# Retention, MoE and SOLU on one core: integer addition and subtractions of the weight conversion on VectorE, the activation as a maximum taken from PSUM

## The chip, the cores and the metric

One core of one Trainium2 chip runs the whole program. TensorE (PE in the profile) multiplies matrices into PSUM; VectorE (DVE), ScalarE (ACT) and GpSimd (POOL) do the elementwise work, and SyncE (SP) issues the transfers. The metric is the device time of one execution in microseconds. A time is a median of several runs.

## The reference, cut to what matters

Three layers follow each other on 3072 tokens of width 512:

```
# retention, 8 heads of 64: a decaying state per head, token by token
state = gamma * state + k_t v_t^T ;  y_t = scale * q_t state
# first feed-forward layer, d_ff 2048
h = x @ w_in
g = where(h >= 1, h, where(h <= -1, 0, (h + 1)**2 / 4))
x = g @ w_out
# second feed-forward layer, d_ff 1024
h = x @ w_in ;  u = h * softmax(h)
out = (layernorm(u) * g_ln) @ w_out
```

The weights come as float64. The kernel turns each weight tile into two float32r parts whose sum is the value, and each product of a weight and an activation is made of three matmuls (high by high, low by high, high by low).

## The kernel before, in words

The program has two phases. Phase A computes retention and the first feed-forward layer together: the 3072 tokens make 8 blocks of 384, and d_ff makes 16 parts of 128, so there are 128 slots (block, part). A slot is `moe_h` (12 matmuls of 384 columns into a PSUM tile `hp`, L325), the activation, and two slots later `moe_out` (12 matmuls into `acc`, L360). Retention (`attention`) goes in between, in steps that a table assigns to slots. Phase B is the second feed-forward layer, 24 tiles of 128 tokens (`h2p`, `tp`, `op`).

Weights are converted in phase A. A weight tile arrives as 128 partitions by 512 float64 (`w_raw`), and `conv_w` makes `m` (tile `wm`) and `p` (tile `wp`) of its two words. ACT takes the high word (L139), DVE clips it (L140), shifts it (L143) and puts the sign in (L144, from `w_raw` and `wm`); ACT makes `p` from the low word (L142); then `m` and `p` are added as 32-bit integers (L145), ACT rounds the sum to the high part (L149), and the low part is the difference (L150). Eight of the last 16 tiles are scaled on the way (L147). There are 48 tiles: 32 for the first layer, taken up over slots 0 to 26 or so, and 16 for the second layer, during the last block of phase A. The choice of engine for L150 is `lo_eng`: of the 48 differences, 14 are on DVE (`LO_I`, `LO_O`) and 34 on POOL; all 48 integer additions are on POOL.

The activation of a slot works on 128x384 values: DVE clips `hp` to -1..1 (L337), ACT makes `rr`, the part of `hp` above 1 (L338), ACT squares the clipped value (L339, half plus half of it), DVE adds the two (L340, `cs` and `rr`, both in SBUF), and `split` rounds the sum on ACT (L121, `gh`) and takes the rest on DVE (L122, `gl`). `hp` is read by L337 and L338; there are two such PSUM tiles, so a slot's `hp` has to be free again when the second slot after it begins.

Order: the program is written in slots, and a list scheduler (a timeline simulation at build time) settles each engine's order from it by priority and readiness. Each engine then runs its own queue in that order and waits on semaphores. So a change of one instruction can move many others.

Of the kernel before, what the change touches and what calls it, by code (L numbers as in the profile page):

```python
# [9 lines left out]
F32 = mybir.dt.float32  # L10
F32R = mybir.dt.float32r
U32 = mybir.dt.uint32
I32 = mybir.dt.int32
AF = mybir.ActivationFunctionType
ALU = mybir.AluOpType
AX = mybir.AxisListType

B, H, S, D = 4, 8, 768, 64
# [8 lines left out]
BLK = 384  # L27
# [3 lines left out]
NF = FF // 128  # L31
NF2 = FF2 // 128
NTILE = NT // 128
# words of the high half of a float64, read as float32: 2^-127 and the largest float32r
LO_I = (0,1)
LO_O = range(4,16)
LO_2 = 0
# [25 lines left out]
C_ACT = 0  # L63
# [10 lines left out]
def kernel(  # L74
# [16 lines left out]
    order = ExitStack()  # L91
    if DMA_ORDER > -99:
        order.enter_context(tc.manual_schedule(engines={mybir.EngineType.SP}))
    ve, sc, gp, pe = nc.vector, nc.scalar, nc.gpsimd, nc.tensor
# [12 lines left out]
    neg1 = const.tile([128, 1], F32, tag="neg1", name="neg1")  # L107
    mask = const.tile([128, 1, C], F32, tag="mask", name="mask")
    half = const.tile([128, 1], F32, tag="half", name="half")
# [4 lines left out]
    def fl(t):  # L114
        return t.bitcast(F32)
# [5 lines left out]
            sc.activation(hi, src, AF.Copy)  # L121
        (lo_eng or ve).tensor_tensor(out=lo, in0=src, in1=fl(hi), op=ALU.subtract)  # L122

# [1 line left out]
    wi, wo = {}, {}  # L125
    state = {}

# [5 lines left out]
    def conv_w(raw, scale=None, lo_eng=None):  # L133
        lw, hw = raw[:, :, 0], raw[:, :, 1]
        m = cv.tile([128, 512], F32, tag="wm", name="wm", bufs=WM_BUFS)
        p = cv.tile([128, 512], F32, tag="wp", name="wp", bufs=WP_BUFS)
        mu, mi = m.bitcast(U32), m.bitcast(I32)
        # the high word, cut to the range of float32, gives sign, exponent and 20 bits
        sc.activation(m, hw.bitcast(F32), AF.Abs)  # L139
        ve.tensor_scalar(m, m, W_MIN, W_MAX, op0=ALU.max, op1=ALU.min)  # L140
        # the low word, rounded to the last 3 bits, lies in the bits of a float32 of 2 upwards
        sc.activation(p, lw, AF.Copy, bias=2.0, scale=2.0 ** -51)  # L142
        ve.tensor_scalar(mu, mu, 3, None, op0=ALU.logical_shift_left)  # L143
        ve.scalar_tensor_tensor(mu, hw, 0x80000000, mu, op0=ALU.bitwise_and, op1=ALU.bitwise_xor)  # L144
        gp.tensor_tensor(out=mi, in0=mi, in1=p.bitcast(I32), op=ALU.add)  # L145
        if scale is not None:
            ve.tensor_scalar(m, m, scale, None, op0=ALU.mult)  # L147
        w = wp.tile([128, 2, 512], F32R, tag="w", name="w")
        sc.activation(w[:, 0, :], m, AF.Copy)  # L149
        (lo_eng or gp).tensor_tensor(out=w[:, 1, :], in0=m, in1=fl(w[:, 0, :]), op=ALU.subtract)  # L150
        return w[:, 0, :], w[:, 1, :]

# [1 line left out]
    # Heads go in pairs (even, odd); the even one takes partitions 0-63 of queries, keys and  # L154
    # state, the odd one 64-127, and TensorE works on both halves of its array at a time.
    # In x the halves of pairs 2 and 3 are swapped, and so are the rows of w_in.
    def attention(u, env):
        b, c = divmod(u, NCH)
        first, last = c == 0, c == NCH - 1
# [94 lines left out]
                gp.tensor_tensor(out=d, in0=d, in1=g, op=ALU.mult)  # L254

    w2i, w2o = {}, {}
# [1 line left out]
    ve.memset(neg1, -1.0)  # L258
    ve.memset(half, 0.5)
    ve.memset(mask, 1.0)  # L260
# [2 lines left out]
    moe = ctx.enter_context(tc.tile_pool(name="moe", bufs=2))  # L263
# [6 lines left out]
    env = {"attp": attp, "xp": xp, "x": {}}  # L270
    GB = 3

    # Phase A goes over (block, part of d_ff) in an order that takes up new weights at half the
    # rate at first, while they are converted; a block's sum may be put aside in DRAM between.
    segs = [(0, 0, SA), (1, 0, SB), (0, SA, NF), (1, SB, NF)] + [(b, 0, NF) for b in range(2, NBLK)]
    slots = [(b, f, f == f0, f == f1 - 1, f0 == 0, f1 == NF)
             for (b, f0, f1) in segs for f in range(f0, f1)]
# [2 lines left out]
        base.setdefault(b, n)  # L280
        first_use.setdefault(f, n)

    # slot -> units of attention that take a step in it
    sched = {}
    for u in range(NU):
        blk, k = divmod(u, CPB)
        x = (k - 3, SA - 3 + k, X2 + 3 * k)[blk] if blk < 3 else base[blk] - NF + PER * k + SHIFT
        at = (x - STEP0, x - 2, x - 1, x) if u < NF32 else (x - 5, x - 3, x - 2, x - 2, x - 1, x)
# [29 lines left out]
    def moe_h(blk, f):  # L318
        xh, xl = env["x"][blk]
        hp = ps_h.tile([128, 512], F32, tag="h", name="hp")[:, :BLK]  # L320
        wh, wl = wi[f]
        n = 0
        for (l, r) in ((wh, xh), (wl, xh), (wh, xl)):
            for k in range(KD):
                pe.matmul(hp, l[:, k * 128:(k + 1) * 128], r[:, k, :], start=(n == 0), stop=(n == 3 * KD - 1))  # L325
                n += 1
        cs = moe.tile([128, BLK], F32, tag="cs", name="cs")
        rr = moe.tile([128, BLK], F32, tag="rr", name="rr", bufs=1)
        gh = moe.tile([128, BLK], F32R, tag="gh", name="gh", bufs=GB)
        gl = moe.tile([128, BLK], F32R, tag="gl", name="gl", bufs=GB)  # L330
        if blk < C_ACT:
            sc.activation(cs, hp, AF.Relu, bias=half, scale=0.5)
            sc.activation(rr, hp, AF.Relu, bias=neg1)
            ve.tensor_scalar(cs, cs, 1.0, None, op0=ALU.min)
            sc.activation(cs, cs, AF.Square)
        else:
            ve.tensor_scalar(cs, hp, -1.0, 1.0, op0=ALU.max, op1=ALU.min)  # L337
            sc.activation(rr, hp, AF.Relu, bias=neg1)  # L338
            sc.activation(cs, cs, AF.Square, bias=half, scale=0.5)  # L339
        ve.tensor_tensor(out=cs, in0=cs, in1=rr, op=ALU.add)  # L340
        split(cs, gh, gl)
        return gh, gl

# [61 lines left out]
    for s, slot in enumerate(slots):  # L405
        blk, f = slot[:2]
# [22 lines left out]
    while pend:  # L429
        moe_out(*pend.pop(0))  # L430

# [1 line left out]
    if True:  # L433
        ident = bp.tile([128, 128], F32, tag="ident", name="ident", bufs=1)
        nc.sync.dma_start(ident, ident_d)
# [20 lines left out]
        def h2(t):  # L456
            hi, lo = x2s.pop(t)
            pool, tag = ((ps_a, "pa"), (ps_acc, "acc"))[1 if PSV else t % 2]
            hps = [pool.tile([128, 512], F32, tag=tag, name="h2p") for _ in range(2)]
            for n in range(2):  # L460
                m = 0
                for (l, part) in ((hi, 0), (hi, 1), (lo, 0)):
                    for k in range(KD):
                        pe.matmul(hps[n], l[:, k, :], w2i[k, n][part], start=(m == 0), stop=(m == 3 * KD - 1))  # L464
                        m += 1
            st = bp.tile([128, 16], F32, tag="st", name="st", bufs=4)
            e = wp.tile([128, 2, 512], F32, tag="w", name="e")
            u = wp.tile([128, 2, 512], F32, tag="w", name="u")
            bn = bp.tile([128, 2, 6], F32, tag="bn", name="bn")
            for n in range(2):  # L470
                ve.tensor_reduce(st[:, n:n + 1], hps[n], axis=AX.X, op=ALU.max)
            ve.tensor_scalar(st[:, 2:3], st[:, 0:1], st[:, 1:2], -1.0, op0=ALU.max, op1=ALU.mult)
            for n in range(2):
                sc.activation(e[:, n, :], hps[n], AF.Exp, bias=st[:, 2:3], accum_out=st[:, 3 + n:4 + n])
            for n in range(2):
                ve.tensor_tensor(out=u[:, n, :], in0=hps[n], in1=e[:, n, :], op=ALU.mult)
                ve.bn_stats(bn[:, n, :], u[:, n, :])
            ve.bn_aggr(st[:, 6:8], bn)
            ve.tensor_scalar(u, u, st[:, 6:7], None, op0=ALU.subtract)
            # f = r / sqrt(r^2 var + eps), r = 1 / (sum + 1e-9)  # L480
            ve.tensor_scalar(st[:, 8:9], st[:, 3:4], st[:, 4:5], 1e-9, op0=ALU.add, op1=ALU.add)
            ve.reciprocal(st[:, 9:10], st[:, 8:9])
            ve.tensor_scalar(st[:, 10:11], st[:, 7:8], st[:, 9:10], st[:, 9:10], op0=ALU.mult, op1=ALU.mult)
            ve.tensor_scalar(st[:, 10:11], st[:, 10:11], 1e-6, None, op0=ALU.add)
            # 1 / sqrt by Newton's steps from a first guess off the exponent
            si = st.bitcast(I32)
            ve.tensor_scalar(si[:, 11:12], si[:, 10:11], 1, None, op0=ALU.arith_shift_right)
            ve.tensor_scalar(si[:, 11:12], si[:, 11:12], -1.0, float(0x5F3759DF), op0=ALU.mult, op1=ALU.add)
            for _ in range(4):
                ve.tensor_scalar(st[:, 13:14], st[:, 10:11], st[:, 11:12], st[:, 11:12], op0=ALU.mult, op1=ALU.mult)  # L490
                ve.tensor_scalar(st[:, 13:14], st[:, 13:14], -0.5, 1.5, op0=ALU.mult, op1=ALU.add)
                ve.tensor_scalar(st[:, 11:12], st[:, 11:12], st[:, 13:14], None, op0=ALU.mult)
            ve.tensor_scalar(st[:, 12:13], st[:, 11:12], st[:, 9:10], None, op0=ALU.mult)
            ust[t] = (u, st)
# [103 lines left out]
```

## Time and profile before

| what | value |
|---|---|
| median of 3 runs | 972.96 us (972.27 to 973.82) |
| span of the profiled execution | 969.7 us |
| PE busy | 936.3 us, 97% |
| DVE busy | 741.9 us, 77% |
| ACT busy | 455.6 us, 47% |
| POOL busy | 201.0 us, 21% |

The profile holds one execution. Its span runs from its first to its last instruction; its own time outside the profiler was not recorded, and the median of the runs is 3.3 us above the span (start and end of the program), so times below are the span plus 3.3 us. Busy time is an average over stages with different limits, which is why the rows below are taken by stage.

### The profile page before, as it was taken

The numbers are of one execution on the slowest core, as the hardware profiler recorded it, in microseconds if no ns is written. First come the engines' busy times: TensorE is split into PE (matmuls) and PEld (weight loads), VectorE is DVE, ScalarE is ACT, GpSimd is POOL, SyncE is SP. The second block draws the span as 40 slices with busy tenths as digits, with TensorE's granted clock in tenths as the row PEclk, the third lists the DMA queues.
The fourth block names the chain that finished last, engine by engine and source line by source line (L and its number), as shares of the span: only waits on it lengthen the run. The fifth ranks groups of instructions, "written<-read, shape, count | busy, mean of one in ns | idle before, by whom it ended". The sixth has DMA issues, their size and how long they took to land.

```text
span 969.7 us, 14961 instructions
## 1 busy us (share of the span) xinstructions
PE 936.3 (97%) x5560; PEld 856.5 (88%) x5560; DVE 741.9 (77%) x1593; ACT 455.6 (47%) x905; POOL 201.0 (21%) x177
## 2 busy tenths in 40 slices
PE   8798898999999999999999999989999999999998
PEld 7588888999999999999999999969888888888886
DVE  6999999877666666655664574997788888888885
ACT  3557676545545545544553464664433333333322
POOL 2754544212211221111220120662000000000000
PEclk9899999999999999999999999999999999999999
DMA  9902823154233232420320230311111011010000
GB/s 366 360 1 82 250 82 114 48 169 126 79 98 116 92 97 80 128 77 22 114 72 12 107 143 1 122 64 69 66 55 42 35 55 54 23 61 28 22 23 33
DMA packets 31465, 87.03 MB, mean 90 GB/s; under 512 B 4384, under 2 KB 10656, under 8 KB 31392
## 3 DMA queue, kind: packets, MB, share of 16 engines
q1 hardware_dynamic: 31392, 86.08, 26.9%
q8 instruction: 44, 0.72, 0.3%
q14 instruction: 29, 0.24, 0.1%
HBM read 71.90 MB, written 14.16 MB: 89 GB/s over the span
## 4 chain that ended last, share of the span: by engine, by line
PE 74%; DVE 18%; issue 3%; ACT 2%; DMA 2%; SPq 0%; POOL 0%; ACTq 0%; DVEq 0%; POOLq 0%
PE acc L360 19%; PE hp L325 19%; PE h2p L464 14%; PE op L516 14%; DVE wm L144 3%; DVE cs L340 3%; DVE wm L140 2%; PE pv L233 2%; PE tp L505 2%; DVE gl L122 2%; PE qp L206 2%; DVE wm L143 2%; DVE cs L337 2%; PE pv L229 2%; DVE w L150 1%
## 5 line engine op out<-in xcount | busy, mean ns | idle before, releaser
L360 PE MATMUL acc<-gh,w 128*128 128x384 f32 x1024 | 214.3, 339 | 9.6 <-ACT gh L121 7.6
L325 PE MATMUL hp<-xh,w 128*128 128x384 f32 x1024 | 209.6, 340 | 5.6 <-ACT rr L338 3.9
L360 PEld LDWEIGHTS acc<-gh,w 128*128 128x128 f32 x1024 | 180.1, 189 | 15.4 <-ACT gh L121 10.4
L325 PEld LDWEIGHTS hp<-xh,w 128*128 128x128 f32 x1024 | 179.0, 189 | 12.2 <-ACT rr L338 6.2
L338 ACT ACTIVATE rr<-hp,neg 128x384 f32<-128x384 f32 x128 | 74.1, 579 | 161.4 <-DVE cs L337 161.2
L340 DVE TENSOR_TENSOR cs<-cs,rr 128x384 f32<-128x384 f32 x128 | 86.0, 672 | 77.7 <-ACT cs L339 76.8
L360 PE MATMUL acc<-gl,w 128*128 128x384 f32 x512 | 121.7, 338 | 4.8 <-DVE gl L122 4.8
L325 PE MATMUL hp<-xl,w 128*128 128x384 f32 x512 | 111.8, 338 | 0.0
L122 DVE TENSOR_TENSOR gl<-cs,gh 128x384 fp32r<-128x384 f32 x128 | 85.5, 668 | 26.7 <-ACT gh L121 24.5
L121 ACT ACTIVATE gh<-cs 128x384 fp32r<-128x384 f32 x128 | 66.8, 522 | 65.7 <-DVE cs L340 65.5
L464 PE MATMUL h2p<-w,x2h 128*128 128x512 f32 x384 | 97.4, 395 | 0.0
L360 PEld LDWEIGHTS acc<-gl,w 128*128 128x128 f32 x512 | 90.3, 188 | 8.1 <-DVE gl L122 7.5
L337 DVE TENSOR_SCALAR cs<-hp 128x384 f32<-128x384 f32 x128 | 70.5, 551 | 32.3 <-PE hp L325 31.8
L325 PEld LDWEIGHTS hp<-xl,w 128*128 128x128 f32 x512 | 91.7, 190 | 0.5 <-DVE xl L122 0.3
L516 PE MATMUL op<-w,lh 128*128 128x512 f32 x384 | 91.4, 390 | 0.2 <-ACT lh L121 0.2
L145 POOL TENSOR_TENSOR wm<-wm,wp 128x512 int32<-128x512 int32 x48 | 69.1, 1440 | 88.0 <-DVE wm L144 70.6
L516 PEld LDWEIGHTS op<-w,lh 128*128 128x128 f32 x384 | 71.9, 188 | 15.4 <-ACT lh L121 0.5
L464 PEld LDWEIGHTS h2p<-w,x2h 128*128 128x128 f32 x384 | 70.5, 188 | 13.5
L339 ACT ACTIVATE cs<-cs,half 128x384 f32<-128x384 f32 x128 | 77.6, 606 | 2.5 <-DVE cs L337 2.5
L150 POOL TENSOR_TENSOR w<-wm,w 128x512 fp32r<-128x512 f32 x34 | 49.6, 1461 | 52.2 <-ACT w L149 51.9
L211 POOL TENSOR_SCALAR_AFFINE_SELECT sm<-sm 128x512 f32<-128x512 f32 x36 | 36.3, 1010 | 99.6 <-DVE sm L210 99.6
L254 POOL TENSOR_TENSOR state<-state,gdec 64x256 f32<-64x256 f32 x32 | 22.0, 688 | 165.1 <-DVE state L253 163.9
(79 smaller groups left out, 1299.7 us busy)
## 6 DMA issues: line engine op xcount, KB each, us to landing
qk<-in_qk_t_dram SPq DMA_DIRECT2D x72, 256.0 KB, 3.8
kv<-in_kv_t_dram SPq DMA_DIRECT2D x24, 512.0 KB, 3.8
w_raw<-in_w_in_dram SPq DMA_DIRECT2D x24, 512.0 KB, 7.3
w_raw<-in_w_out_dram SPq DMA_DIRECT2D x24, 512.0 KB, 6.7
x2d<-xs SPq DMA_DIRECT2D x32, 192.0 KB, 2.0
x2r<-x2d SPq DMA_DIRECT2D x8, 768.0 KB, 4.3
out_dram<-o SPq DMA_DIRECT2D x24, 256.0 KB, 2.0
qn<-in_qk_t_dram SPq DMA_DIRECT2D x15, 256.0 KB, 3.1
```

Source lines behind the costliest of these rows:

```text
L121: sc.activation(hi, src, AF.Copy)
L122: (lo_eng or ve).tensor_tensor(out=lo, in0=src, in1=fl(hi), op=ALU.subtract)
L145: gp.tensor_tensor(out=mi, in0=mi, in1=p.bitcast(I32), op=ALU.add)
L150: (lo_eng or gp).tensor_tensor(out=w[:, 1, :], in0=m, in1=fl(w[:, 0, :]), op=ALU.subtract)
L325: pe.matmul(hp, l[:, k * 128:(k + 1) * 128], r[:, k, :], start=(n == 0), stop=(n == 3 * KD - 1))
L337: ve.tensor_scalar(cs, hp, -1.0, 1.0, op0=ALU.max, op1=ALU.min)
L338: sc.activation(rr, hp, AF.Relu, bias=neg1)
L339: sc.activation(cs, cs, AF.Square, bias=half, scale=0.5)
L340: ve.tensor_tensor(out=cs, in0=cs, in1=rr, op=ALU.add)
L360: pe.matmul(acc[d][:, :BLK], l[:, d * 128:(d + 1) * 128], r, start=(first and m == 1), stop=(last and m == 3))
L464: pe.matmul(hps[n], l[:, k, :], w2i[k, n][part], start=(m == 0), stop=(m == 3 * KD - 1))
L516: pe.matmul(op, l[:, f, :], w2o[f][part], start=(n == 0), stop=(n == 3 * NF2 - 1))
```

## The change

The integer addition L145 and the remaining subtractions L150 are issued on DVE in place of POOL. In the activation, `rr` goes away with its ACT instruction, and the last step becomes a maximum of `hp`, read from PSUM, and the squared value. (For h above 1 the squared value is 1 and the maximum is h; below -1 it is 0; in between the square is never below h.) The branch on `C_ACT`, which is 0, was never taken before and is gone. All else in the diff is comments.

```
-        gp.tensor_tensor(out=mi, in0=mi, in1=p.bitcast(I32), op=ALU.add)
+        ve.tensor_tensor(out=mi, in0=mi, in1=p.bitcast(I32), op=ALU.add)
         if scale is not None:
             ve.tensor_scalar(m, m, scale, None, op0=ALU.mult)
         w = wp.tile([128, 2, 512], F32R, tag="w", name="w")
         sc.activation(w[:, 0, :], m, AF.Copy)
-        (lo_eng or gp).tensor_tensor(out=w[:, 1, :], in0=m, in1=fl(w[:, 0, :]), op=ALU.subtract)
+        ve.tensor_tensor(out=w[:, 1, :], in0=m, in1=fl(w[:, 0, :]), op=ALU.subtract)
...
         cs = moe.tile([128, BLK], F32, tag="cs", name="cs")
-        rr = moe.tile([128, BLK], F32, tag="rr", name="rr", bufs=1)
...
-            ve.tensor_scalar(cs, hp, -1.0, 1.0, op0=ALU.max, op1=ALU.min)
-            sc.activation(rr, hp, AF.Relu, bias=neg1)
-            sc.activation(cs, cs, AF.Square, bias=half, scale=0.5)
-        ve.tensor_tensor(out=cs, in0=cs, in1=rr, op=ALU.add)
+        ve.tensor_scalar(cs, hp, -1.0, 1.0, op0=ALU.max, op1=ALU.min)
+        sc.activation(cs, cs, AF.Square, bias=half, scale=0.5)
+        ve.tensor_tensor(out=cs, in0=hp, in1=cs, op=ALU.max)
         split(cs, gh, gl)
```

Eight lines less stand above, so in the changed program L337, L339 and L340 are L331, L332 and L333, and what stood at L360 is at L353.

In DVE's queue, around the fifth to seventh slot of phase A (before: the conversion of `wm_925` and `wm_975`, with slot work between), the rows read:

```order
L140 TENSOR_SCALAR wm_925<-wm_925 128x512
L337 TENSOR_SCALAR cs_809<-hp_796 128x384
L143 TENSOR_SCALAR wm_925<-wm_925 128x512
L122 TENSOR_TENSOR gl_754<-cs_751,gh_753 128x384
L144 SCALAR_TENSOR_TENSOR wm_925<-w_raw_736,wm_925 128x512
L140 TENSOR_SCALAR wm_975<-wm_975 128x512
L143 TENSOR_SCALAR wm_975<-wm_975 128x512
L340 TENSOR_TENSOR cs_809<-cs_809,rr_810 128x384
L144 SCALAR_TENSOR_TENSOR wm_975<-w_raw_792,wm_975 128x512
```

and in the changed program at about the same place (`wm_543` and `wm_636` are two tiles in conversion; `wp` is their other word):

```order
L143 TENSOR_SCALAR wm_636<-wm_636 128x512
L144 SCALAR_TENSOR_TENSOR wm_543<-w_raw_389,wm_543 128x512
L150 TENSOR_TENSOR w_488<-wm_480,w_488 128x512
L144 SCALAR_TENSOR_TENSOR wm_636<-w_raw_413,wm_636 128x512
L333 TENSOR_TENSOR cs_660<-hp_647,cs_660 128x384
L145 ISA wm_543<-wm_543,wp_544 128x1024
L145 ISA wm_636<-wm_636,wp_637 128x1024
L122 TENSOR_TENSOR gl_662<-cs_660,gh_661 128x384
L150 TENSOR_TENSOR w_551<-wm_543,w_551 128x512
L150 TENSOR_TENSOR w_644<-wm_636,w_644 128x512
```

Additions and differences now stand in DVE's queue between the other steps, a few places behind the step that feeds them. The addition is built as another instruction than before: it goes over 1024 elements of two bytes in place of 512 of four. The last step of the activation reads `hp`.

In POOL's queue the same stretch of the program reads, before:

```order
L145 TENSOR_TENSOR wm_925<-wm_925,wp_926 128x512
L145 TENSOR_TENSOR wm_975<-wm_975,wp_976 128x512
L150 TENSOR_TENSOR w_933<-wm_925,w_933 128x512
L145 TENSOR_TENSOR wm_986<-wm_986,wp_987 128x512
L150 TENSOR_TENSOR w_994<-wm_986,w_994 128x512
L145 TENSOR_TENSOR wm_1034<-wm_1034,wp_1035 128x512
```

and in the changed program POOL holds only retention's own steps there:

```order
L183 TENSOR_TENSOR kv_307<-kv_307,vdec_88 128x512
L254 TENSOR_TENSOR state_105<-state_105,gdec_89 64x4x64 x2
L183 TENSOR_TENSOR kv_1336<-kv_1336,vdec_88 128x512
L211 AFFINE_SELECT sm_1474<-sm_1474 128x512
L211 AFFINE_SELECT sm_1552<-sm_1552 128x512
L183 TENSOR_TENSOR kv_1492<-kv_1492,vdec_88 128x512
```

The 82 instructions of the conversion have left this queue, and 82 have come into DVE's.

## Rows read from the trace of the kernel before

**Rows 1.** Busy us (and instructions) of each engine by stage of the span.
```profile
core 0: us, PE busy (x) PEld busy (x) DVE busy (x) ACT busy (x) POOL busy (x), PEclk, DMA share, GB/s
...
25.00:185.00 160.00, 142.37 (x837) 128.98 (x838) 153.30 (x228) 102.34 (x193) 81.70 (x61) 0.96 0.41 138
...
200.00:590.00 390.00, 389.50 (x2593) 378.12 (x2592) 250.20 (x458) 193.67 (x394) 70.99 (x74) 1.00 0.31 94
...
616.00:668.00 52.00, 45.36 (x239) 40.59 (x238) 50.18 (x69) 32.46 (x59) 32.25 (x22) 1.00 0.27 99
...
700.00:970.00 270.00, 265.97 (x1264) 221.75 (x1264) 222.69 (x715) 83.16 (x178) 0.00 (x0) 1.00 0.11 39
```

**Rows 2.** Groups on DVE from 25 to 185 us: count, busy us, mean ns.
```profile
L144 DVE SCALAR_TENSOR_TENSOR wm<-w_raw,wm 128x512 uint32<-128x512 uint32 x30 | 25.6, 854 | 0.2
L122 DVE TENSOR_TENSOR gl<-cs,gh 128x384 fp32r<-128x384 f32 x26 | 22.1, 851 | 2.4 <-ACT gh L121 2.3
L340 DVE TENSOR_TENSOR cs<-cs,rr 128x384 f32<-128x384 f32 x26 | 20.8, 801 | 2.8 <-ACT cs L339 2.7
L143 DVE TENSOR_SCALAR wm<-wm 128x512 uint32<-128x512 uint32 x29 | 20.6, 713 | 0.2
L140 DVE TENSOR_SCALAR wm<-wm 128x512 f32<-128x512 f32 x29 | 19.1, 663 | 0.1
L150 DVE TENSOR_TENSOR w<-wm,w 128x512 fp32r<-128x512 f32 x14 | 15.8, 1129 | 0.0
...
L199 DVE TENSOR_TENSOR kh<-qk,kh 64x512 fp32r<-64x512 f32 x7 | 5.8, 843 | 0.2
L122 DVE TENSOR_TENSOR xl<-xt,xh 128x512 fp32r<-128x512 f32 x4 | 5.0, 1252 | 0.0
L200 DVE TENSOR_TENSOR qs<-qk,qs 128x512 fp32r<-128x512 f32 x5 | 4.6, 923 | 0.1
```

**Rows 3.** Timeline of DVE from 106 us: start us, duration us.
```profile
106.06 0.68 DVE L144 SCALAR_TENSOR_TENSOR wm<-w_raw,wm 128x512 uint32<-128x512 uint32 x1
106.66 0.41 DVE L140 TENSOR_SCALAR wm<-wm 128x512 f32<-128x512 f32 x1
107.11 1.38 DVE L143 TENSOR_SCALAR wm<-wm 128x512 uint32<-128x512 uint32 x1
108.53 1.67 DVE L144 SCALAR_TENSOR_TENSOR wm<-w_raw,wm 128x512 uint32<-128x512 uint32 x1
...
111.88 0.68 DVE L150 TENSOR_TENSOR w<-wm,w 128x512 fp32r<-128x512 f32 x1
112.61 0.56 DVE L122 TENSOR_TENSOR gl<-cs,gh 128x384 fp32r<-128x384 f32 x1
...
114.11 0.43 DVE L143 TENSOR_SCALAR wm<-wm 128x512 uint32<-128x512 uint32 x1
```

**Rows 4.** Timeline of POOL in the same stretch.
```profile
106.91 1.30 POOL L145 TENSOR_TENSOR wm<-wm,wp 128x512 int32<-128x512 int32 x1 [1.78 <-ACT w L149]
108.17 1.48 POOL L150 TENSOR_TENSOR w<-wm,w 128x512 fp32r<-128x512 f32 x1
```

**Rows 5.** Groups over the whole span: DVE steps that read PSUM, and ACT's `rr`.
```profile
L337 DVE TENSOR_SCALAR cs<-hp 128x384 f32<-128x384 f32 x128 | 70.5, 551 | 32.3 <-PE hp L325 31.8
...
L338 ACT ACTIVATE rr<-hp,neg 128x384 f32<-128x384 f32 x128 | 74.1, 579 | 161.4 <-DVE cs L337 161.2
...
L373 DVE TENSOR_TENSOR xs<-acc,xs 128x384 f32<-128x384 f32 x8 | 4.3, 552 | 3.4 <-DMA xs<-x2p 2.5 <-PE qp L206 1.0
```

**Rows 6.** Groups on POOL from 25 to 185 us.
```profile
L145 POOL TENSOR_TENSOR wm<-wm,wp 128x512 int32<-128x512 int32 x30 | 43.1, 1439 | 55.1 <-DVE wm L144 42.9 <-ACT cs L339 8.3 <-ACT w L149 1.8
L150 POOL TENSOR_TENSOR w<-wm,w 128x512 fp32r<-128x512 f32 x18 | 26.4, 1465 | 9.7 <-ACT w L149 9.5
```

**Rows 7.** Groups on POOL from 616 to 668 us.
```profile
L150 POOL TENSOR_TENSOR w<-wm,w 128x512 fp32r<-128x512 f32 x12 | 17.7, 1474 | 6.0 <-ACT w L149 5.9
L145 POOL TENSOR_TENSOR wm<-wm,wp 128x512 int32<-128x512 int32 x10 | 14.8, 1481 | 12.0 <-DVE wm L144 12.0
```

More of the change, by code (lines that the diff above doesn't have):

```diff
@@ L327, in moe_h @@
         cs = moe.tile([128, BLK], F32, tag="cs", name="cs")
-        rr = moe.tile([128, BLK], F32, tag="rr", name="rr", bufs=1)
         gh = moe.tile([128, BLK], F32R, tag="gh", name="gh", bufs=GB)
         gl = moe.tile([128, BLK], F32R, tag="gl", name="gl", bufs=GB)
-        if blk < C_ACT:
-            sc.activation(cs, hp, AF.Relu, bias=half, scale=0.5)
-            sc.activation(rr, hp, AF.Relu, bias=neg1)
-            ve.tensor_scalar(cs, cs, 1.0, None, op0=ALU.min)
-            sc.activation(cs, cs, AF.Square)
-        else:
-            ve.tensor_scalar(cs, hp, -1.0, 1.0, op0=ALU.max, op1=ALU.min)
-            sc.activation(rr, hp, AF.Relu, bias=neg1)
-            sc.activation(cs, cs, AF.Square, bias=half, scale=0.5)
-        ve.tensor_tensor(out=cs, in0=cs, in1=rr, op=ALU.add)
+        ve.tensor_scalar(cs, hp, -1.0, 1.0, op0=ALU.max, op1=ALU.min)
+        sc.activation(cs, cs, AF.Square, bias=half, scale=0.5)
+        ve.tensor_tensor(out=cs, in0=hp, in1=cs, op=ALU.max)
         split(cs, gh, gl)
```

## The prediction

> **What bounds the kernel now.** I read the windows by stage first, because the page's averages (PE 97%, DVE 77%) hide that the bound changes along the span. From 200 to 590 us PE is busy 389.5 of 390 us and DVE 250 [rows 1]: there PE's matmuls set the time and nothing that this change does to DVE, ACT or POOL can show. From 700 us on POOL does nothing, DVE is busy 222.7 and PE 266.0 of 270 us [rows 1]; the change touches no instruction there. Two stages are different. From 25 to 185 us, while the first layer's weights are converted, DVE is busy 153.3 of 160 us and PE only 142.4; from 616 to 668 us, while the second layer's are, DVE is busy 50.2 of 52 us and PE 45.4 [rows 1]. In both DVE sets the pace, so the question is whether DVE gets more or less to do in these 212 us.
>
> At first sight more: 82 instructions come to the engine that is full. But the groups on DVE show that it is full of something else. One conversion step, L143, takes 713 ns in the mean between 25 and 185 us, L150 takes 1129 [rows 2]; the timeline shows the same forms at 0.43 and 0.68 us where they run free [rows 3]. The long ones can be matched: L143 begins at 107.11 and takes 1.38 us, while POOL's L145 runs from 106.91 to 108.21; L144 begins at 108.53 and takes 1.67 us, while POOL's L150 runs from 108.17 to 109.65 [rows 3, 4]. So they end about 0.3 to 0.55 us after POOL's end, as if most of their work began only then. The DVE forms that read PSUM keep their price with POOL busy or not: L337 551 ns, L373 552 [rows 5]. A POOL instruction of 1.44 us [rows 6] thus costs DVE time too.
>
> **The change, part by part.**
>
> Stretch before, 25 to 185 us: count by (mean less free duration), from [rows 2] and [rows 3], with 0.68 us for all two-source forms of 512, 0.56 for those of 384, 0.43 for L143, 0.41 for L140. L144 30 x 0.174 = 5.2; L122 `gl` 26 x 0.291 = 7.6; L340 26 x 0.241 = 6.3; L143 29 x 0.283 = 8.2; L140 29 x 0.253 = 7.3; L150 14 x 0.449 = 6.3; L199, `xl` and L200 together 7 x 0.163 + 4 x 0.572 + 5 x 0.243 = 4.6. Sum 45.5 us, in a stage of 160.
>
> What goes: POOL is busy 81.7 us there [rows 1], of which the additions and differences are 43.1 + 26.4 = 69.5 [rows 6]. The rest, 12.2 us or 15%, is retention's and stays. If the stretch follows POOL's time, 6.8 us stay and 38.7 go.
>
> What comes: 30 additions and 18 differences [rows 6]. A difference is known: 0.68 us [rows 3]. In the queue a step of this size puts the next one off by 0.60 us where that one does not depend on it (106.06 to 106.66), and by 0.73 us at worst (111.88 to 112.61) [rows 3]; I take 0.60, since the changed queue alternates between tiles. The addition has no row: it is built as another instruction, over 1024 elements of two bytes. Lower bound: it moves the same bytes as a two-source form of 512 words, 0.68 us. Upper bound: it goes at the pace of single elements; from 384 to 512 elements a two-source form grows from 0.56 to 0.68 us [rows 3], so 0.94 ns each, and 1024 take 0.68 + 0.48 = 1.16 us; POOL's own 1.44 us [rows 6] is further off. I take 0.68, since the fast forms (L140: 512 words in 0.41) show that DVE need not spend a step per element, and it is the row of the same bytes. 48 x 0.60 = 28.8 us.
>
> The Trainium skill, VectorE: DVE Perf Modes, section "Mode 2×_1P", says that two-source forms of 16-bit elements go two per cycle; with the 151 cycles at 0.96 GHz that the page puts on top of a two-source addition, an estimate for 1024 is 0.69 us, and the sum would stay as it is. No row of this trace has a two-byte form of that kind.
>
> Net in this stage: DVE's demand falls by 38.7 - 28.8 = 9.9 us. Not all of it comes back as time: DVE's 153.3 then stands at 143, beside PE's 142.4, and two engines so close wait for each other in turn. I take seven tenths, 7 us. If each step costs 0.73 instead, 38.7 - 35.0 = 3.7 us are left.
>
> From 616 to 668 us: POOL is busy 32.25 us, all conversion [rows 1, 7]. At the first stage's ratio (45.5 / 81.7 = 0.56) that is 18 us of stretch, and all of it goes. 10 additions and 12 differences come [rows 7]: 22 x 0.60 = 13.2 us. Net 4.8 us less; PE's idle 52 - 45.4 = 6.6 us is the ceiling. I take 4.
>
> The activation: ACT loses 128 `rr` of 579 ns, 74 us [rows 5]. ACT is busy 102 of 160 and 32 of 52 us [rows 1], so that is no time by itself; in the two stages it shortens the way from `hp` to `gh` by one instruction, which DVE's in-order queue mostly covers with conversion work. From 200 to 590 us PE's 389.5 of 390 us cover it wholly. The new last step reads one source from PSUM and one from SBUF: 0.55 us like L373 [rows 5], as much as L340 where it runs free, and it can't be stretched (counted above). What it costs: `hp` stays occupied until DVE's last step, about one ACT step and one DVE step longer than when `rr` was its last reader (0.58 + 0.55 us [rows 5]). There are two such tiles, and between the end of one slot's `moe_h` and the second next one stand 36 matmuls, so this is nothing unless DVE lags; where it lags, PE waits anyway. I put it at 0, bound 3 us.
>
> The Trainium skill, VectorE: DVE Perf Modes, section "The TRN2 errata", speaks against this step: 120 fixed cycles from PSUM and 58 from SBUF, so an estimate of 65 ns more for each maximum, 1.7 us over the 26 slots of the first stage [rows 2], and the sum would be 9.3 us in place of 11. The trace disagrees: 552 ns for L373 from PSUM [rows 5], 0.56 us for `gl` of the same shape from SBUF [rows 3].
>
> The other eight additions and four differences (48 - 40 and 34 - 30) lie outside the two stages, where DVE is not full, and their stretch goes with them: 0.
>
> Sum: 7 + 4 = 11 us. Span 969.7 - 11 = 958.7, plus 3.3 = **962.0 us**.
>
> **The rivals.**
>
> *The addition costs a step per element.* 0.48 us more on each of the 40 additions in the two stages is 19 us; DVE's demand then rises by 19.2 - (9.9 + 4.8) = 4.5 us, up to as much again goes to waits in a fuller queue, and the time is 977 to 982. It decides above 0.68 + 14.7 / 40 = 1.05 us an addition. For it: the instruction's 1024 elements; against: the bytes are the same. This is the slower side; 0.09.
>
> *The waits move to DVE.* POOL no longer waits for ACT before L150 (9.5 us on 18 [rows 6]); DVE does, and behind each waiting step stands the next slot's L331, for which PE waits in the end. 0.2 us on each of 70 moved steps is 14 us and eats the gain: 968 to 975. Against: in the changed queue two or three steps of other tiles stand between an addition and its difference, more than ACT's rounding takes. 0.16.
>
> *PE becomes the bound at once.* If the shorter activation and the freed DVE remove all waits in both stages, PE's idle time, 17.6 + 6.6 us [rows 1], goes: 949 to 955. For it: demand on DVE falls to PE's level; against: slots with much conversion stay above it. 0.12.
>
> *The stretch is not POOL's.* If long DVE steps came from something else, 28.8 + 13.2 = 42 us of work would come and nothing go: about 1015. The matched pairs [rows 3, 4] speak against it. 0.03.
>
> **How the numbers follow.** The forecast, 955 to 968, has 0.60. This kernel's runs can tell 0.2% (2 us) from no change. Faster: 0.60 + 0.12, and 0.08 of the waiting case: 0.80. Same: 0.06 of that case. Slower: 0.02 of it, 0.09 and 0.03: 0.14. The range leaves out the slow cases and the fastest tip: 951 to 975.
>
> **What would show it.** From 25 to 185 us DVE's L140, L143, L144 and `gl` near 0.42, 0.43, 0.68 and 0.56 us; the addition near 0.68; the maximum at 0.55; POOL near 12 us; the first conversion stage over some 7 us earlier, the second 4 us shorter; from 200 us on the same length. It would be wrong if the addition takes over 1 us, if DVE's idle time in these stages grows by more than 10 us, or if DVE's steps stay long without POOL.

## The result and the profile after

The changed kernel takes 947.64 us (median of 4 runs, 945.66 to 949.32) beside 972.62 us for the kernel before: a ratio of 0.9732, 95% interval 0.9706 to 0.9759. It is 25.0 us faster. The direction was forecast, the size was not: 11 us, and 947.6 lies below the range. The profiled execution has a span of 947.5 us, 22.2 less than before. A run's time lies 1.7 to 2.0 us above its span wherever both are recorded (here 949.32 and 947.5), so the 3.3 us that were put down to start and end of the program are in part scatter: the profiled execution of the kernel before took some 971.5 us, a little under its median, and that of the changed kernel is the slowest of its four. The stages below therefore add up to 22.2 us and not to 25.0. The page of the changed kernel, its busy times and its chain by engine:

```profile
PE 927.9 (98%) x5560; PEld 858.6 (91%) x5560; DVE 718.2 (76%) x1675; ACT 401.3 (42%) x777; POOL 80.3 (8%) x95
...
PE 89%; DVE 7%; DMA 2%; issue 1%; ACT 0%; SPq 0%; DVEq 0%; ACTq 0%
```

and the chain of the kernel before:

```profile
PE 74%; DVE 18%; issue 3%; ACT 2%; DMA 2%; SPq 0%; POOL 0%; ACTq 0%; DVEq 0%; POOLq 0%
```

DVE has 82 instructions more and is busy 23.7 us less (741.9 before); in the chain DVE's share fell from 18% to 7% and PE's rose from 74% to 89%. To see where the time went, both spans are cut where the same work is done: at the ends of the 28th, the 118th and the 128th slot's `moe_h`. The windows of the kernel before, cut there:

```profile
core 0: us, PE busy (x) PEld busy (x) DVE busy (x) ACT busy (x) POOL busy (x), PEclk, DMA share, GB/s
0.00:185.00 185.00, 162.69 (x1057) 146.84 (x1058) 170.95 (x263) 110.49 (x205) 88.53 (x73) 0.96 0.48 169
185.00:623.00 438.00, 437.50 (x2882) 425.80 (x2881) 285.45 (x516) 222.77 (x448) 84.55 (x85) 1.00 0.30 91
623.00:675.50 52.50, 45.86 (x243) 41.09 (x242) 47.02 (x67) 29.59 (x55) 27.92 (x19) 1.00 0.19 72
675.50:969.70 294.20, 290.22 (x1384) 242.81 (x1383) 238.46 (x750) 92.71 (x198) 0.00 (x0) 1.00 0.11 41
```

and those of the changed kernel (the instruction counts of PE show that the cuts are the same to within two matmuls):

```profile
0.00:175.70 175.70, 160.76 (x1058) 149.42 (x1059) 159.85 (x316) 101.51 (x181) 17.92 (x23) 0.95 0.51 178
175.70:611.70 436.00, 435.33 (x2881) 424.79 (x2880) 280.29 (x529) 183.66 (x357) 62.42 (x72) 1.00 0.31 92
611.70:653.30 41.60, 41.60 (x241) 41.60 (x241) 40.40 (x84) 25.36 (x45) 0.00 (x0) 1.00 0.26 91
653.30:947.50 294.20, 290.23 (x1384) 242.81 (x1383) 237.70 (x748) 90.81 (x194) 0.00 (x0) 1.00 0.12 41
```

So 9.3 us come from the first stage, 2.0 from the long middle, 10.9 from the ten slots of the second conversion stage, and none from phase B. In the first stage DVE is busy 11.1 us less with 53 instructions more. In the second PE is now busy all the time. The groups on DVE from 25 to 172 us, which answer to [rows 2] (count, busy us, mean ns):

```profile
L144 DVE SCALAR_TENSOR_TENSOR wm<-w_raw,wm 128x512 uint32<-128x512 uint32 x31 | 22.3, 723 | 0.2
L150 DVE TENSOR_TENSOR w<-wm,w 128x512 fp32r<-128x512 f32 x32 | 22.2, 702 | 0.0
L145 DVE CUSTOM_DVE_ANT_0 wm<-wm,wp 128x1024 uint16<-128x1024 uint16 x31 | 21.1, 689 | 0.0
L122 DVE TENSOR_TENSOR gl<-cs,gh 128x384 fp32r<-128x384 f32 x25 | 14.5, 580 | 0.0
...
L333 DVE TENSOR_TENSOR cs<-hp,cs 128x384 f32<-128x384 f32 x26 | 14.4, 556 | 0.3 <-ACT cs L332 0.3
L143 DVE TENSOR_SCALAR wm<-wm 128x512 uint32<-128x512 uint32 x30 | 13.6, 453 | 0.0
L140 DVE TENSOR_SCALAR wm<-wm 128x512 f32<-128x512 f32 x29 | 12.7, 441 | 0.1
```

Every step that was long before is short now: L144 723 ns (854), `gl` 580 (851), L143 453 (713), L140 441 (663), L150 702 (1129). The addition, the one price that no row of before had, is 689 ns.

With the two elements a cycle that the Trainium skill, VectorE: DVE Perf Modes, section "Mode 2×_1P", gives for 16-bit elements, the prediction's estimate for it was 0.69 us; this measurement agrees.

### The profile page after: what moved, and what is told of

The parts are those of the page before. It is cut to its first block, busy times and chain, and to the rows that moved or that the text cites. A ratio compares the mean times of both kernels' runs of the same rounds, so it can differ in the third digit from the quotient of the medians.

```text
span 947.5 us, 14776 instructions
## 1 busy us (share of the span) xinstructions
PE 927.9 (98%) x5560; PEld 858.6 (91%) x5560; DVE 718.2 (76%) x1675; ACT 401.3 (42%) x777; POOL 80.3 (8%) x95
## 4 chain that ended last, share of the span: by engine, by line
PE 89%; DVE 7%; DMA 2%; issue 1%; ACT 0%; SPq 0%; DVEq 0%; ACTq 0%
PE hp L325 26%; PE acc L353 26%; PE h2p L457 14%; PE op L509 14%; PE pv L233 2%; PE tp L498 2%; PE qp L206 2%; PE pv L229 2%; PE sp L245 1%; DVE wm L144 1%; DVE wm L145 1%; DMA xs<-x2p 1%; DVE w L150 1%; DMA kv<-in_kv_t_dram 1%; DVE wm L140 1%
## 5 line engine op out<-in xcount | busy, mean ns | idle before, releaser
L325 PE MATMUL hp<-xh,w 128*128 128x384 f32 x1024 | 212.2, 341 | 7.3 <-DVE cs L333 3.5
L353 PE MATMUL acc<-gh,w 128*128 128x384 f32 x1024 | 208.9, 335 | 4.0 <-ACT gh L121 3.6
L353 PEld LDWEIGHTS acc<-gh,w 128*128 128x128 f32 x1024 | 179.4, 188 | 5.7 <-ACT gh L121 4.2
L332 ACT ACTIVATE cs<-cs,half 128x384 f32<-128x384 f32 x128 | 78.9, 617 | 166.0 <-DVE cs L331 165.6
L353 PE MATMUL acc<-gl,w 128*128 128x384 f32 x512 | 120.2, 336 | 0.4 <-DVE gl L122 0.4
L331 DVE TENSOR_SCALAR cs<-hp 128x384 f32<-128x384 f32 x128 | 71.2, 557 | 49.9 <-PE hp L325 49.1
L333 DVE TENSOR_TENSOR cs<-hp,cs 128x384 f32<-128x384 f32 x128 | 71.4, 558 | 43.4 <-ACT cs L332 42.6
L122 DVE TENSOR_TENSOR gl<-cs,gh 128x384 fp32r<-128x384 f32 x128 | 78.3, 612 | 34.1 <-ACT gh L121 33.5
L353 PEld LDWEIGHTS acc<-gl,w 128*128 128x128 f32 x512 | 90.9, 188 | 1.5 <-issue 0.7
L467 ACT ACTIVATE e<-h2p,st 128x512 f32<-128x512 f32 x48 | 32.6, 686 | 49.8 <-DVE st L484 38.3
L457 PE MATMUL h2p<-w,x2l 128*128 128x512 f32 x192 | 51.4, 390 | 0.0
L509 PE MATMUL op<-w,ll 128*128 128x512 f32 x192 | 47.7, 390 | 0.0
L464 DVE TENSOR_REDUCE st<-h2p 128x1 f32<-128x512 f32 x48 | 33.2, 691 | 19.0 <-PE h2p L457 18.9
L121 ACT ACTIVATE x2h<-x2r 128x512 fp32r<-128x512 f32 x24 | 15.1, 631 | 76.0 <-PE h2p L457 53.1
```

Source lines behind the costliest of these rows:

```text
L333: ve.tensor_tensor(out=cs, in0=hp, in1=cs, op=ALU.max)
L353: pe.matmul(acc[d][:, :BLK], l[:, d * 128:(d + 1) * 128], r, start=(first and m == 1), stop=(last and m == 3))
L509: pe.matmul(op, l[:, f, :], w2o[f][part], start=(n == 0), stop=(n == 3 * NF2 - 1))
```

## Experiments

Two theories were put to the test. The theory of ports (a port is an engine's access to SBUF): a POOL instruction holds up DVE's steps that take two sources from SBUF, or one source in a fast form, and the gain is this stretch less the work that DVE takes over. The theory of chains: what helps is that steps follow each other faster, the conversion without POOL's 1.44 us steps, the activation with one ACT step less. Each ratio is against the kernel before, run beside it on the same chip.

**The conversion alone.** The activation of before (`rr` on ACT, L340 from SBUF) with the conversion on DVE; the edit against the kernel before:

```
-        gp.tensor_tensor(out=mi, in0=mi, in1=p.bitcast(I32), op=ALU.add)
+        ve.tensor_tensor(out=mi, in0=mi, in1=p.bitcast(I32), op=ALU.add)
...
-        (lo_eng or gp).tensor_tensor(out=w[:, 1, :], in0=m, in1=fl(w[:, 0, :]), op=ALU.subtract)
+        ve.tensor_tensor(out=w[:, 1, :], in0=m, in1=fl(w[:, 0, :]), op=ALU.subtract)
```

> The conversion of the changed kernel (additions and differences on DVE) with the activation of before (rr on ACT, the sum on DVE from two SBUF sources). Ports theory (POOL's conversion steps hold up DVE's SBUF steps, and the gain is that stretch less the work added): POOL has almost nothing left in the two conversion stages, so the sum L340 runs free at 0.56 us even from SBUF and nearly the whole gain is there, 948 to 953 us. Chain theory (the gain comes from shorter chains, among them the one ACT step less from hp to gh): the activation's share is missing, 955 to 962 us.

945.56 us, ratio 0.971 (0.9686 to 0.9735). The whole gain is here, and the activation of the changed kernel adds nothing to it. The time lies 2 us under the range of the ports theory and 9 us under that of the chains.

**The activation alone.** The maximum from PSUM, the conversion as before.

> The activation of the changed kernel with the conversion of before (82 steps on POOL). Ports theory: only the stretch of L340 goes, some 6 us of DVE's demand in the first stage and 4 in the second, all other steps stay stretched: 962 to 970 us, the maximum at 0.56 us. Chain theory: every slot's chain is one ACT step (0.58 us) shorter, 955 to 962 us. If the stretch is of no matter: 972 us.

972.15 us, ratio 0.9993 (0.9973 to 1.0013): nothing. Both theories expected more; the number is the one written down for the case that the stretch is of no matter. DVE's rows show something else, that the stretch did not go away. Groups on DVE from 25 to 186 us, and the window of the first stage at the same cut as above:

```profile
L144 DVE SCALAR_TENSOR_TENSOR wm<-w_raw,wm 128x512 uint32<-128x512 uint32 x31 | 26.9, 869 | 0.3
L140 DVE TENSOR_SCALAR wm<-wm 128x512 f32<-128x512 f32 x29 | 23.1, 800 | 0.1
L122 DVE TENSOR_TENSOR gl<-cs,gh 128x384 fp32r<-128x384 f32 x26 | 22.9, 880 | 1.5 <-ACT gh L121 1.2
L143 DVE TENSOR_SCALAR wm<-wm 128x512 uint32<-128x512 uint32 x30 | 21.1, 703 | 0.3
L332 DVE TENSOR_TENSOR cs<-hp,cs 128x384 f32<-128x384 f32 x27 | 14.8, 549 | 2.6 <-ACT cs L331 2.5
...
L150 DVE TENSOR_TENSOR w<-wm,w 128x512 fp32r<-128x512 f32 x14 | 13.9, 990 | 0.0
```

```profile
0.00:186.20 186.20, 164.67 (x1058) 148.73 (x1059) 170.23 (x266) 99.96 (x181) 88.94 (x73) 0.95 0.49 168
```

The maximum is never held up (549 ns, from 801 [rows 2]), but L140 goes from 663 to 800, `gl` from 851 to 880 and L144 from 854 to 869. Of what one step is spared, the steps behind it pay a good part: L140, `gl` and L144 together 29 x 0.137 + 26 x 0.029 + 31 x 0.015 = 5.2 us more, L150 and L143 14 x 0.139 + 30 x 0.010 = 2.2 less, so 3.0 against the 26 x 0.252 = 6.6 us spared. With all of DVE's steps counted its busy time in the first stage stayed nearly the same, 170.2 us after 171.0. POOL still has its 82 instructions, and DVE meets them at another place in its queue. A second reason may lie in the longer hold of `hp`. PE's waits for it from 25 to 185 us, first in the kernel before, then here:

```profile
PE hp L325 <- ACT rr L338: 2.7, 3, 1.4
```

```profile
PE hp L325 <- DVE cs L332: 7.1, 5, 2.8
```

No run parts the two.

**POOL kept busy for nothing.** The changed kernel, and behind each converted weight one or two additions on POOL (82 in all, as many as have left it) into a tile that nobody reads.

```
+        for _ in range(1 if lo_eng else 2):
+            gp.tensor_tensor(out=dz, in0=fl(w[:, 0, :]), in1=fl(w[:, 0, :]), op=ALU.add)
         return w[:, 0, :], w[:, 1, :]
```

> The changed kernel, and POOL runs 82 additions of 128x512 float32 besides, one or two behind each converted weight, into a tile that nobody reads. It is extra work that no engine waits for. Ports theory: some 39 us of stretch in the first stage and 20 in the second come back on top of the added DVE work, 985 to 1005 us, slower than before; L140 and L143 rise from 0.43 to about 0.65 to 0.75 us in the mean. Chain theory: nobody waits for POOL, 946 to 950 us.

981.72 us, ratio 1.0087 (1.0055 to 1.0119): 34 us slower than the changed kernel and 9 us slower than the kernel before, by work that no engine waits for (in its trace no wait of PE, DVE or ACT ends with POOL). The chain theory has no place for this. DVE's groups from 25 to 196 us (an added line moves the numbers by one) and the windows at the same cuts as above:

```profile
L151 DVE TENSOR_TENSOR w<-wm,w 128x512 fp32r<-128x512 f32 x32 | 31.4, 988 | 0.1
L145 DVE SCALAR_TENSOR_TENSOR wm<-w_raw,wm 128x512 uint32<-128x512 uint32 x30 | 24.3, 814 | 0.1
...
L144 DVE TENSOR_SCALAR wm<-wm 128x512 uint32<-128x512 uint32 x29 | 19.2, 661 | 0.0
L123 DVE TENSOR_TENSOR gl<-cs,gh 128x384 fp32r<-128x384 f32 x26 | 17.3, 666 | 0.2 <-ACT gh L122 0.2
L141 DVE TENSOR_SCALAR wm<-wm 128x512 f32<-128x512 f32 x29 | 16.3, 566 | 0.1
L334 DVE TENSOR_SCALAR cs<-hp 128x384 f32<-128x384 f32 x27 | 14.7, 547 | 0.7 <-PE hp L328 0.7
```

```profile
0.00:196.10 196.10, 168.30 (x1058) 153.55 (x1059) 186.61 (x313) 100.74 (x179) 79.25 (x73) 0.93 0.45 159
...
633.20:685.20 52.00, 45.69 (x242) 42.80 (x241) 52.00 (x88) 26.16 (x46) 28.80 (x19) 0.97 0.23 82
```

The long steps are back, and only those that read SBUF: the clip of `hp`, L334, keeps its 547 ns. The first stage is 20.4 us longer than in the changed kernel, the second 10.4. The expectation (59 us together) was too high: the dummies stretch DVE less than the conversion did, and each of the long steps is shorter than before (566 ns for L141, 663 for L140 before [rows 2]). The granted clock is lower as well, 0.93 (0.95 in the changed kernel) and 0.97 (1.00); by these shares that is some 6.5 us at most (an estimate: 196.1 x 0.07 less 175.7 x 0.05, and 52 x 0.03), far less than the loss.

The Trainium skill, SBUF — State Buffer, section "Who interferes with whom", says that DVE's second pair of SBUF ports is shared with GpSimd and locked for an instruction, against two-source and fast one-source forms but not against other forms with at most one SBUF source. The runs agree: 661 ns for L144 here against 453 for the same step (L143) without the dummies, 547 for the clip from PSUM.

**The addition twice.** A second integer addition, of zeros, behind each.

> The changed kernel with a second integer addition (of zeros) behind each of the 48, so an addition costs 1.38 us of DVE in place of 0.69, a little more than the upper bound of the prediction (1.16). If DVE is still the bound in the two stages: 30 x 0.6 = 18 us in the first and 10 x 0.6 = 6 in the second, 965 to 972 us. If PE has become the bound and DVE has slack, much less: 950 to 957 us. The prediction's rival put 1.16 us at 977 to 982.

966.73 us, ratio 0.9931 (0.9904 to 0.9958), at 0.7 us of DVE more for each of 48 tiles. Its windows:

```profile
0.00:191.80 191.80, 164.77 (x1071) 153.87 (x1072) 174.65 (x345) 102.75 (x179) 19.38 (x23) 0.94 0.47 160
...
627.40:669.00 41.60, 41.60 (x242) 41.60 (x241) 41.00 (x84) 23.61 (x41) 0.00 (x0) 1.00 0.16 53
669.00:964.60 295.60, 290.37 (x1384) 242.68 (x1382) 242.88 (x759) 93.48 (x199) 0.00 (x0) 1.00 0.13 46
```

The first stage grows by 16.1 us: there DVE is still the bound after the change. The ten slots at the end stay at 41.6 us with PE busy throughout, but not because DVE has room: it is busy 41.0 us of them with 84 instructions, as many as in the changed kernel, and the added work that does not fit slips behind the cut, where DVE has 11 instructions more and the stage is 1.4 us longer (294.2 in the changed kernel). So the prediction's rival, an addition of 1.16 us, would not have made the kernel slower; with twice the 0.69 us it is still ahead of the kernel before.

**Each half on POOL again.** The changed kernel with the 34 differences, or with the 48 additions, back on POOL.

```
-        ve.tensor_tensor(out=w[:, 1, :], in0=m, in1=fl(w[:, 0, :]), op=ALU.subtract)
+        (lo_eng or gp).tensor_tensor(out=w[:, 1, :], in0=m, in1=fl(w[:, 0, :]), op=ALU.subtract)
```

> The changed kernel with the 34 differences back on POOL; the additions stay on DVE. Ports theory, at the ratio of before (0.56 us of stretch for each us of POOL): first stage 26 us of POOL are 15 us of stretch, less 18 x 0.6 = 11 us of work that leaves DVE, so 4 us longer; second stage 10 - 7 = 3 us more demand, under the slack that the doubled addition showed there (6 us and more), so 0. Together 950 to 953 us. If a difference on POOL cost DVE nothing, the kernel would gain: 936 to 940 us.

> The changed kernel with the 48 integer additions back on POOL; all differences stay on DVE. Ports theory: first stage 43 us of POOL are 24 us of stretch, less 30 x 0.6 = 18, so 6 us longer; second stage 8 - 6 = 2 us, under the slack. Together 952 to 956 us. If the gain hung on the additions alone (the chain through POOL between L144 and L149): all of it is lost, 968 to 973 us; if on the differences alone: 948 us.

949.78 us (ratio 0.9756, 0.9733 to 0.978) and 956.24 us (0.9826, 0.9806 to 0.9846). Both lie within 0.3 us of the ranges of the ports theory, but not by its working. The first stage and the ten slots, with the differences on POOL:

```profile
0.00:172.10 172.10, 159.86 (x1057) 148.15 (x1058) 158.35 (x293) 99.21 (x179) 42.57 (x41) 0.96 0.51 179
...
609.30:657.40 48.10, 43.55 (x241) 41.28 (x241) 44.36 (x76) 26.21 (x45) 12.69 (x9) 1.00 0.23 79
```

and with the additions:

```profile
0.00:178.90 178.90, 161.79 (x1058) 151.04 (x1059) 161.23 (x284) 101.23 (x181) 64.92 (x55) 0.94 0.50 175
...
614.90:659.90 45.00, 43.00 (x241) 41.40 (x241) 41.60 (x75) 25.72 (x45) 10.88 (x8) 1.00 0.22 79
```

With the differences on POOL the ten slots take 6.5 us more than in the changed kernel, where nothing was expected for a slack of 6 us that DVE did not have, and the first stage is not the expected 4 us longer. With the additions the two are 3.4 and 3.2 us longer, where 0 and 6 were expected. That the totals came out is luck. Taken back alone the additions cost 8.6 us and the differences 2.1 (which is within the scatter of the runs); both at once, which is the kernel with the activation alone, cost 24.5. In the ten slots the two costs add up (6.5 and 3.4, beside 10.9 for the kernel before). In the first stage they do not: one half on POOL costs 3 us or nothing, both cost 9.3 us (the kernel before) to 10.5 (the activation alone), and why is open. The first stage of one kernel differs by some 4 us between executions (171.3 to 175.7 us for the conversion alone), so the 3.6 us less with the differences on POOL mean nothing.

**Fewer DVE steps in the activation.** ACT takes relu and square, DVE one step that reads PSUM.

```
-        ve.tensor_scalar(cs, hp, -1.0, 1.0, op0=ALU.max, op1=ALU.min)
-        sc.activation(cs, cs, AF.Square, bias=half, scale=0.5)
-        ve.tensor_tensor(out=cs, in0=hp, in1=cs, op=ALU.max)
+        sc.activation(cs, hp, AF.Relu, bias=half, scale=0.5)
+        sc.activation(cs, cs, AF.Square)
+        ve.scalar_tensor_tensor(cs, cs, 1.0, hp, op0=ALU.min, op1=ALU.max)
```

> The changed kernel with the activation in two steps on ACT (relu of half plus half of hp, then its square) and one on DVE (minimum with 1, then maximum with hp from PSUM), so DVE has two steps a slot in place of three; the same function. If DVE's demand sets the first stage: 26 x 0.5 = 13 us less demand there, of which PE's own pace leaves 6 to 10 us: 937 to 942 us. If PE has become the bound everywhere: 946 to 948 us. The hold of hp stays as long as in the changed kernel.

936.37 us, ratio 0.9633 (0.9613 to 0.9653): 11 us better than the changed kernel, 0.6 us under the range that was given for DVE's demand, and the best of all. The first stage is where it falls:

```profile
0.00:163.20 163.20, 154.32 (x1068) 145.26 (x1069) 146.91 (x289) 110.53 (x209) 18.64 (x23) 0.99 0.55 192
...
597.90:639.50 41.60, 41.60 (x241) 41.60 (x241) 36.26 (x73) 28.66 (x54) 0.00 (x0) 1.00 0.26 91
```

28 slots in 163.2 us after 175.7, DVE busy 146.9 after 159.9; the end stage stays at PE's 41.6. The granted clock rose with it, 0.99 (0.95 in the changed kernel), and no run parts what that gives from what the fewer steps give.

**Does the maximum from PSUM cost something?** The conversion alone had come out at 945.6, so it was run again beside the changed kernel, and then beside a kernel with `rr` behind the square, which holds `hp` an ACT step longer.

> The conversion on DVE with the activation of before, once more and with more rounds beside the changed kernel. If the maximum from PSUM costs time because hp is held until DVE's last step: 945 to 946 us and 1 to 3 us below the changed kernel in the same job. If the two activations are the same: no difference, 946 to 948 us both.

> The changed kernel itself, as the partner of the two others in the same job: 946 to 949 us. Held hp: 1 to 3 us above the kernel with the activation of before; no difference otherwise.

> The conversion on DVE with the activation of before, but ACT takes rr behind the square in place of ahead of it: the same work, and hp stays held one ACT step (0.6 us) longer. If holding hp is what costs the changed kernel 2 to 4 us: 946 to 949 us. If the hold is of no matter and the order of the queues at the start makes the difference: 943 to 946 us, as with rr first, or a difference of either sign.

> The conversion on DVE with the activation of before, as the partner of the kernel with rr last in the same job: 942 to 946 us.

In the first pair 944.2 us (942.4 to 945.8) for the activation of before and 947.97 (946.59 to 949.16) for the changed one: 3.8 us, and the two spreads do not overlap. In the second pair 947.91 (946.19 to 949.65) with `rr` last and 945.51 (942.2 to 948.81) with `rr` first, which overlap. The changed kernel's TensorE around its seventh slot:

```profile
65.43 0.86 PE L353 MATMUL acc<-gl,w 128*128 128x384 f32 x4
69.50 1.90 PE L353 MATMUL acc<-gh,w 128*128 128x384 f32 x8 [3.21 <-ACT gh L121]
71.19 3.61 PE L325 MATMUL hp<-xh,w 128*128 128x384 f32 x12
...
76.90 0.68 PE L353 MATMUL acc<-gl,w 128*128 128x384 f32 x3
80.44 2.49 PE L325 MATMUL hp<-xh,w 128*128 128x384 f32 x8 [2.86 <-DVE cs L333]
```

PE waits 2.86 us there for the maximum to give `hp` back, and 3.21 us for `gh` before; with the activation of before PE waits 0.2 us for `rr` in its whole repeated run. The stretch from 25 to 90 us in the first pair, the changed kernel and then the activation of before:

```profile
25.00:90.00 65.00, 55.63 (x330) 49.85 (x331) 62.20 (x123) 38.41 (x67) 4.99 (x6) 0.89 0.37 142
```

```profile
25.00:90.00 65.00, 55.65 (x348) 48.96 (x349) 62.90 (x125) 43.25 (x78) 4.99 (x6) 0.97 0.41 155
```

That holding `hp` costs some 2 to 4 us is what all four runs point to. But the granted clock is lower in the changed kernel (0.89 and 0.97), the step that holds `hp` and the place that the scheduler gives it change together, and the run with the longer hold alone does not stand clear of its partner. It stays open.

## Why the prediction was right or wrong

**The mechanism was right.** POOL's conversion steps stretched DVE's, the stretch went with them, and DVE, with 82 instructions more, had less to do. The dummies show it: POOL's work alone, with no one waiting, takes the gain away again. The conversion alone has the whole gain.

**The prices were right.** Of the stretch some 37 us went by the six large groups of [rows 2] (38.7 predicted, with the small ones). The addition 0.69 us (0.68 taken, 1.16 the upper bound), the difference 0.70, the maximum 0.56 (0.55) and never stretched. DVE's demand in the first stage fell by 11.1 us (9.9 predicted), in the last ten slots by 6.6 (4.8 predicted over 52 us).

**The step that failed is the one from demand to time, above all in the second stage.** "PE's idle 52 - 45.4 = 6.6 us is the ceiling. I take 4": it gave 10.9. The ceiling was read from PE's busy time, and that is not PE at its pace. Before, 243 matmuls were shown busy for 45.86 us; after, 241 take 41.60 us without a gap. So 4.2 us of what the profile called busy before was lost pace, and the ceiling of these slots was 52.5 - 41.6 = 10.9 us. The kernel before shows that pace itself, in the ten slots just ahead:

```profile
581.40:623.00 41.60, 41.60 (x242) 41.60 (x241) 27.04 (x42) 24.21 (x45) 11.30 (x8) 1.00 0.18 58
```

In the disturbed slots the weight loads (PEld) told it too: busy 41.1 of the 52.5 us, where the matmuls show 45.9. All of the 10.9 us was reached, because with the stretch gone DVE just fits into PE's time (40.4 of 41.6 us); with either half back on POOL it no longer does (48.1 and 45.0 us). Of the 14.0 us between the forecast 11 and the measured 25.0, 6.9 are this stage's, 2.3 the first stage's, 2.0 the middle's, and 2.8 lie between the medians and the two profiled executions.

**The first stage** was sized by "seven tenths" of DVE's 9.9 us because DVE's remaining time came close to PE's busy 142.4 us. It gave 9.3 of 11.1, eight tenths; with executions 4 us apart this is no clear miss. PE's busy time was no floor here either: in the 28 slots it is 162.7 us before and 154.3 with fewer DVE steps in the activation, part of it by the granted clock (0.96 and 0.99). The doubled addition lengthens this stage by 16.1 us for 31 x 0.69 = 21 us of work, so DVE is still the bound there.

**The middle**, 2.0 us shorter, was put at 0. PE is busy almost without a gap in both (437.5 of 438.0, 435.3 of 436.0 us) on the same number of matmuls. No run here settles where these 2 us come from.

**The activation** was put at 0 with a bound of 3 us for the longer hold of `hp`. Alone it changes nothing (0.9993), and beside the new conversion the hold may cost 2 to 4 us. The stretch of L340, counted as gain (6.3 us), was no gain by itself: with POOL as before, DVE's busy time in the first stage and the kernel's time did not move.

**The rivals.** *PE becomes the bound at once*, 949 to 955 us, comes nearest, with its ceiling too low for the same reason: it is true for the second stage, not for the first. *The waits move to DVE*: the changed kernel has 0.3 us of waiting on ACT before L333 and none shown before L150, so no. *The addition costs a step per element*: it does not, 0.69 us against 1.16. *The stretch is not POOL's*: the dummies bring it back, so it is.

## What to carry to other kernels

Before you move work off a full engine, look at how long the same instruction takes where its neighbours are quiet: if a large part of the full engine's time is stretch, bringing work over can make it emptier. Take the room that the other engine leaves from its pace in an undisturbed stretch (24 matmuls of a slot in 4.16 us), not from its busy share in the disturbed one. And sparing one step from being held up was worth nothing here while POOL's work stayed; taking that work away was worth the whole gain.

## What the runs showed of the hardware

- A DVE form that reads one source from PSUM and one from SBUF kept a mean of 549 to 558 ns for 128x384 in every run that has one, also while POOL was busy nearly half the time; single steps of the same size from two SBUF sources took 0.55 to 1.65 us in the kernel before. The Trainium skill, VectorE: DVE Perf Modes, section "The TRN2 errata", has PSUM sources dearer by 62 cycles; here 556 ns with a PSUM source in the changed kernel stand beside 0.56 us for `gl`, from SBUF alone, where it runs free [rows 3], and the measurement decides.
- The addition of 32-bit integers, 128x512, takes 689 ns on DVE and ran as 1024 two-byte elements; on POOL it took 1439 ns [rows 6].
- Work that nobody waits for can cost 34 us in 948: 82 dummy additions on POOL.
- In the changed kernel the granted clock stands at the lower of its two levels (1.2 and 2.4 GHz) from 70.8 to 74.2 us and from 81.0 to 84.4 us, each time shortly after a wait of PE has ended (3.21 us up to 69.50, 2.86 us up to 80.44). Behind the first, 12 matmuls take 3.61 us in place of 2.08. So these two waits cost more than their own length:

```profile
70.80:74.20 3.40, 3.40 (x13) 3.40 (x12) 3.33 (x8) 3.35 (x6) 0.00 (x0) 0.50 0.01 2
74.20:81.00 6.80, 3.94 (x23) 3.62 (x22) 5.48 (x12) 4.53 (x9) 0.00 (x0) 1.00 0.00 0
81.00:84.40 3.40, 3.40 (x13) 3.40 (x12) 3.40 (x8) 2.36 (x6) 0.00 (x0) 0.50 0.00 0
```
